# Where the state's decay is applied in a linear-attention and mixture kernel, and in what order its start is laid out

## The chip, the cores and the metric

One core of a Trainium2 chip runs the whole program. The metric is the device time of one execution in microseconds (us); lower is better. The times named are medians of several runs, and one further execution was taken with the profiler.

## The reference

Three layers follow one another. The first is linear attention with a decaying state, for 2 batches, 8 heads, 768 steps and head size 48. Then come a mixture of 4 experts (384 to 1024 to 384, relu) weighted by normalised probabilities, and one wide layer (384 to 2048 to 384, elu). All is float32.

```python
state = np.zeros((B, H, D, D))
for t in range(S):
    kt, vt, rt = (k[:, :, t], v[:, :, t], r[:, :, t])
    cur = np.einsum('bhd,bhe->bhde', u[None] * kt, vt)
    y[:, :, t] = np.einsum('bhd,bhde->bhe', rt, state + cur)
    state = w[None, :, :, None] * state + np.einsum('bhd,bhe->bhde', kt, vt)
...
p = domain_probs / (domain_probs.sum(-1, keepdims=True) + 1e-09)
for e in range(E):
    h = np.maximum(x @ w1[e], 0.0)
    out += p[:, e:e + 1] * (h @ w2[e])
...
h = x @ w_in
g = np.where(h > 0.0, h, np.exp(np.minimum(h, 0.0)) - 1.0)
return g @ w_out
```

The decays w lie between 0.85 and 0.95.

## The kernel before, in words

**The attention** (class Fast) cuts the 1536 steps into 12 chunks of 128, six for each batch. Two tables are made at the start: T holds the powers of w from 0 to 128 (T[:, :, P:P + 1] is w to the 128th), Kd their reciprocals. Receptances are multiplied by T and keys by Kd (s1h, VectorE, L206), so that within a chunk the decay falls out of the product (s2, TensorE, L263). VectorE's copy_predicated (s2p, L270) writes the causal part of it into a tile A that GpSimd (L242) or ScalarE (s1e, L248) has filled with the diagonal term of u. The chunk's own sum over keys and values (s3u, TensorE, L285) goes into a bank pu, with keys from kp, which GpSimd makes in s1k (L216) from the table Kt. Kt is Kd transposed on TensorE (setup_kt, L199) and copied by ScalarE (L200). VectorE then makes the state (s3s): for chunk 0 it multiplies pu by w to the 128th into the padded tile Sp (L302); afterwards it adds the old state to pu (Z, L309) and multiplies by w to the 128th (S, L311). Chunk 1 takes its state from Sp (s3f, L375), later chunks from S (s3, L325), and s3 adds the products of A and v (L334); ScalarE copies the result to yT (L341).

**The layers** (class Gen) work in float32 split in two parts, high and low: ScalarE casts the high part and another engine subtracts it. For weights these are wh (ScalarE, L532) and wl (VectorE, sometimes GpSimd, L533), for activations xh and xl (L495, L496), for the hidden values hh and hl (L696, L697). A group is a first product into a bank ph (st1, L684), its evacuation to hh and hl, and, two groups later, a second product (st2, L722). For the first 1024 steps a group has 256 columns and the two banks ph0 and ph1 take turns (new_ph, counter nph).

**The order.** The program is scheduled by hand: each engine gets its instructions in the order in which the program issues them. The function fast writes that order out: the warm-up matmuls on a tile of zeros (warm, L102), zeros, loads, tables, the first two chunks, and then the layers, between whose groups the steps of the later chunks are dealt out by hand. After the first group (f=0) come a1(2), probs2 and a2(3), after the second a3(2), after the third a1p(3), after the fourth a3(3). After each group's steps, work() issues one split of a weight slice: wh on ScalarE, wl on VectorE. So a3(2), which holds s3s(2), stands before the split of the second group on both engines.

Of the kernel before, what the change touches and what calls it, by code (L numbers as in the profile page):

```python
# [10 lines left out]
F32 = mybir.dt.float32  # L11
# [5 lines left out]
AF = mybir.ActivationFunctionType  # L17
ALU = mybir.AluOpType
# [4 lines left out]
P = 128  # L23
B, H, S, D = 2, 8, 768, 48
NP = H // 2
NCB = S // P
# [8 lines left out]
WARM = 18  # L35
# [15 lines left out]
class Fast:  # L51
# [7 lines left out]
    def __init__(self, g, ctx):  # L59
        self.g, nc, tc = g, g.nc, g.tc  # L60
        self.c = ctx.enter_context(tc.tile_pool(name="at_c", bufs=1))
        self.p2 = ctx.enter_context(tc.tile_pool(name="at_2", bufs=2))
        self.p3 = ctx.enter_context(tc.tile_pool(name="at_3", bufs=3))
        self.p4 = ctx.enter_context(tc.tile_pool(name="at_4", bufs=4))
        self.ps = ctx.enter_context(tc.tile_pool(name="at_ps", bufs=1, space=PSUM))
        c = self.c
        self.A = [c.tile([P, 2, NP, P], F32, name=f"A{i}") for i in range(2)]
        self.kp = [c.tile([P, NP, 2, 64], F32, name=f"kp{i}") for i in range(2)]
        self.Sb = [c.tile([P, NP, 64], F32, name=f"S{i}") for i in range(2)]
        self.wd = c.tile([P, NP], F32, name="wd")  # L70
        self.T = c.tile([P, NP, P + 1], F32, name="T")
        self.Kd = c.tile([P, NP, P], F32, name="Kd")
        self.Kt = c.tile([P, NP, 2, 64], F32, name="Kt")
        self.ub = c.tile([P, DM], F32, name="ub")
        self.ur = c.tile([1, DM], F32, name="ur")
        self.one = c.tile([1, P], F32, name="one")
        self.vp = c.tile([P, 112 + 160 * H], F32, tag="xs", name="vp")
        self.Sp = c.tile([P, 96 + 192 * NP], F32, tag="yT", name="Sp")
        self.mask = c.tile([P, P], U8, name="mask")
        self.rkT, self.rk, self.v, self.va, self.pa, self.st, self.px = ({} for _ in range(7))  # L80
        self.S = self.Sv = self.zero = None

        self.own = [(self.ps, f"pa{i}") for i in range(3)] + [(g.pop, "po2")]
        self.banks = self.own[:3] + [(g.pop, f"po{i}") for i in range(KD)] + [(g.php, "ph0")]
        self.nbank = 0
        self.xd = g.dr.tile([DM, N], F32, name="xd")
# [108 lines left out]
    def setup_kt(self):  # L195
        g, nc = self.g, self.g.nc
        pk = self.bank()
        for p in range(NP):
            nc.tensor.transpose(pk[:, p * P:(p + 1) * P], self.Kd[:, p, :], g.ident)  # L199
        nc.scalar.copy(self.Kt.rearrange("t p j d -> t (p j d)"), pk)  # L200


# [87 lines left out]
    def s3s(self, ci, pu):  # L290
        nc = self.g.nc
        if pu is None:
            return
        old, v = self.Sv, nc.vector
        w = self.T[0:112, :, P:P + 1]
        src = pu[0:112, 0:NP * D].rearrange("q (p e) -> q p e", p=NP)
        if not ci:
            self.Sv = self.Sp[0:112, 96:].rearrange("q (p n) -> q p n", p=NP)[:, :, 0:96].rearrange(
                "q p (j e) -> q p j e", j=2)
            for j in range(2):  # L300
                a = slice(64 * j, 64 * j + D)
                v.tensor_tensor(out=self.Sv[a, :, j, :], in0=src[a], in1=w[a].to_broadcast([D, NP, D]), op=ALU.mult)  # L302
            return
        self.S = self.Sb[ci % 2]
        self.Sv = self.S[0:112, :, 0:D]
        if ci % NCB:
            z = self.p2.tile([P, NP, D], F32, tag="Z", name="Z")[0:112]
            for a, o in [(slice(0, 64), old[:, :, 0]), (slice(64, 112), old[:, :, 1])] if ci == 1 else [(slice(0, 112), old)]:
                v.tensor_tensor(out=z[a], in0=src[a], in1=o[a], op=ALU.add)  # L309
            src = z  # L310
        v.tensor_tensor(out=self.Sv, in0=src, in1=w.to_broadcast([112, NP, D]), op=ALU.mult)  # L311

    def s3(self, ci, more=False):
        g, nc = self.g, self.g.nc
        st = self.st.pop(ci)
        A, v, c = self.A[ci % 2], self.v[ci], ci % NCB
        py = [self.bank()[:, 0:2 * P].rearrange("q (s t) -> q s t", s=2) for j in range(2)]
        heads = [(p, j) for q in range(2) for p in (q, q + 2) for j in range(2)]
        at = lambda p, j, m: py[j][64 * (p // 2):64 * (p // 2) + m, p % 2, :]


        if c:
            for p, j in heads:
                a, m = 64 * j, D if p // 2 else 64
                nc.tensor.matmul(  # L325
                    at(p, j, m), self.S[a:a + D, p, 0:m], st["r"][a:a + D, p, :], start=not p % 2, stop=False)
        if more:
            self.s2(ci + 1)
        pu = self.s3u(ci, g.new_ph() if ci > 2 else g.pop.tile([P, TB], F32, tag="po1", name="po1")) if c < NCB - 1 else None
        for j in range(2):  # L330
            for p in (0, 2, 1, 3):

                h, m = 2 * p + j, D if c or p // 2 else 64
                nc.tensor.matmul(  # L334
                    at(p, j, m), v[:, h * D:h * D + m], A[:, j, p, :], start=not c, stop=not c or p % 2 == 1)
        self.s3s(ci, pu)
        o = (ci % 2) * P
        if not o:
            self.yT = self.c.tile([P, 2, 2, 2 * P], F32, tag="yT", name="yT")
        for j in range(2):  # L340
            nc.scalar.copy(self.yT[0:112, :, j, o:o + P], py[j][0:112])  # L341
        if o:

            t0 = (ci - 1) * P
            for a in range(2):
                nc.sync.dma_start(
                    out=self.xd[:, t0:t0 + 2 * P].rearrange("(a h e) t -> a e h t", a=2, e=D)[a],
                    in_=self.yT[64 * a:64 * a + D].rearrange("e s j t -> e (s j) t"))
            self.xs = self.c.tile([P, KD, 2 * P], F32, tag="xs", name="xs")
            nc.sync.dma_start(out=self.xs, in_=self.xd[:, t0:t0 + 2 * P].rearrange("(k p) t -> p k t", p=P))  # L350
# [127 lines left out]
class Gen:  # L478
# [378 lines left out]
    def fast(self):  # L857
        tc, nc = self.tc, self.nc
        with ExitStack() as ctx:
# [1 line left out]
            self.hp, self.hw = ctx.enter_context(tc.tile_pool(name="hp", bufs=3)), 256  # L861
            actx = ExitStack()
            at = Fast(self, actx)
            at.warm(WARM - 4)
            at.setup_zeros()
            at.setup_loads()
            dp = self.probs_in()
            make_identity(nc, self.ident)
            self.load_next()
            at.load_rk(2)  # L870
# [2 lines left out]
            at.load_v(2)  # L873
            at.setup_masks()
            at.setup_tables()
            at.setup_rest()
            at.setup_tables2()

            def load(c):
                if c < NCH:  # L880
                    at.load_T(c)
                    at.load_v(c)
# [38 lines left out]
            self.probs(dp)  # L921
            at.s1d(2)
            at.s3s(1, pu)
            self.weng = nc.gpsimd
            self.work(0.1)
            self.weng = nc.vector
            at.banks, at.nbank = at.own, 0
            load(4)
            at.load_rk(4)

# [163 lines left out]
```

## Time and profile before

| | |
|---|---|
| median of 3 runs | 653.62 us (653.33 to 654.23) |
| the profiled execution | 653.03 us |
| its span, first to last instruction | 651.1 us |
| mean granted TensorE clock | 0.997 |
| TensorE / VectorE / ScalarE / GpSimd busy | 639.2 / 334.1 / 216.7 / 214.6 us |

Positions in time are microseconds from the start of the span. PE is TensorE, PEld its weight loads, DVE is VectorE, ACT ScalarE, POOL GpSimd; a q behind the name is the engine's sequencer. In a timeline a line gives the start, the time to the end of the last instruction merged into it, the engine, the line of the program, the operation, the tiles it writes and reads with their shapes, and how many instructions were merged. In brackets stand the idle time ahead of it and what ended it.

### The profile page before, as it was taken

What the parts mean: (1) busy time and instruction counts of PE and PEld (TensorE: products, weight loads), DVE (VectorE), ACT (ScalarE), POOL (GpSimd) and SP (SyncE); (2) the same over time, 40 slices, a digit from 0 to 9 for tenths busy, and PEclk for the clock granted to TensorE, in tenths of its full rate; (3) what the DMA queues carried; (4) which work ended last, traced back from release to release, by engine and by line L of the source; (5) the groups of instructions that cost most, each with busy time, mean ns of one, the idle gap of its engine ahead of it and who ended that gap; (6) DMA issues with size and microseconds to landing.
All of it is one profiled execution on the core that took longest, in us unless ns stands there. A gap on an engine that the chain in (4) does not pass through costs nothing.

```text
span 651.1 us, 9435 instructions
## 1 busy us (share of the span) xinstructions
PE 639.2 (98%) x3825; PEld 537.1 (82%) x3825; DVE 334.1 (51%) x472; ACT 216.7 (33%) x370; POOL 214.6 (33%) x178
## 2 busy tenths in 40 slices
PE   9799999999999999999999999999999999999996
PEld 6699998988888888888888888888888888888885
DVE  7975665346454545554545456566667553222221
ACT  5532222333211132211122112123645564544441
POOL 7954773100031212130311122242754434333331
PEclk9999999999999999999999999999999999999998
DMA  8883562343230233421216231318441342001011
GB/s 257 248 288 120 160 175 76 144 122 122 72 97 1 98 120 118 159 88 48 98 49 229 92 138 52 97 35 312 188 146 44 102 145 98 0 1 49 1 49 53
DMA packets 27735, 73.10 MB, mean 112 GB/s; under 512 B 3154, under 2 KB 8580, under 8 KB 27684
## 3 DMA queue, kind: packets, MB, share of 16 engines
q1 hardware_dynamic: 22928, 59.80, 28.6%
q10 hardware_dynamic: 4756, 12.61, 5.1%
q8 instruction: 32, 0.52, 0.3%
q14 instruction: 19, 0.16, 0.1%
HBM read 55.47 MB, written 16.93 MB: 111 GB/s over the span
## 4 chain that ended last, share of the span: by engine, by line
PE 95%; DVE 3%; issue 1%; ACT 0%; DVEq 0%
PE ph L684 45%; PE po L722 45%; PE pa L263 1%; PE ph L102 1%; PE pa L334 1%; PE pa L325 1%; DVE rkT L206 1%; PE po L334 1%; PE ph L285 1%; DVE A L270 0%; DVE wl L533 0%; DVE a L232 0%; DVE acc L772 0%; DVE hl L697 0%; DVE xl L496 0%
## 5 line engine op out<-in xcount | busy, mean ns | idle before, releaser
L722 PE MATMUL po<-hh,wh 128*128 128x512 f32 (+1 forms) x480 | 177.4, 370 | 0.0
L722 PE MATMUL po<-hl,wh 128*128 128x512 f32 (+1 forms) x480 | 176.5, 368 | 0.0
L722 PE MATMUL po<-hh,wl 128*128 128x512 f32 (+1 forms) x480 | 176.5, 368 | 0.0
L684 PE MATMUL ph<-xh,wh 128*128 128x512 f32 (+1 forms) x480 | 174.5, 369 | 1.5 <-DVE xl L496 0.8
L684 PE MATMUL ph<-xh,wl 128*128 128x512 f32 (+1 forms) x480 | 173.8, 368 | 0.0
L696 ACT ACTIVATE hh<-ph 128x512 fp32r<-128x512 f32 (+1 forms) x112 | 60.2, 537 | 269.3 <-PE ph L684 266.4
L697 DVE SCALAR_TENSOR_TENSOR hl<-ph,hh 128x512 fp32r<-128x512 f32 (+1 forms) x112 | 68.5, 613 | 154.6 <-ACT hh L696 154.2
L684 PE MATMUL ph<-xl,wh 128*128 128x512 f32 (+1 forms) x480 | 124.6, 368 | 0.0
L684 PEld LDWEIGHTS ph<-xh,wh 128*128 128x128 f32 x480 | 90.4, 188 | 17.6 <-DVE hl L697 1.0
L722 PEld LDWEIGHTS po<-hh,wh 128*128 128x128 f32 x480 | 90.4, 188 | 16.5 <-issue 1.5
L722 PEld LDWEIGHTS po<-hl,wh 128*128 128x128 f32 x480 | 90.4, 188 | 15.0
L722 PEld LDWEIGHTS po<-hh,wl 128*128 128x128 f32 x480 | 90.4, 188 | 15.0
L684 PEld LDWEIGHTS ph<-xh,wl 128*128 128x128 f32 x480 | 90.5, 188 | 14.9
L709 POOL TENSOR_TENSOR hl<-g,hh 128x512 fp32r<-128x512 f32 x48 | 63.2, 1318 | 117.4 <-ACT hh L708 109.3
L684 PEld LDWEIGHTS ph<-xl,wh 128*128 128x128 f32 x480 | 85.9, 188 | 15.2 <-DVE xl L496 0.2
L595 POOL TENSOR_TENSOR nl<-a,wide 128x768 fp32r<-128x768 f32 x16 | 29.9, 1870 | 173.5 <-issue 105.8
L706 DVE SCALAR_TENSOR_TENSOR g<-m,ph 128x512 f32<-128x512 f32 x48 | 33.0, 686 | 104.4 <-ACT m L704 100.1
L744 POOL TENSOR_TENSOR acc<-acc,t 128x512 f32<-128x512 f32 x27 | 34.2, 1297 | 72.8 <-DVE t L743 72.8
L708 ACT CAST hh<-g 128x512 fp32r<-128x512 f32 x48 | 29.9, 622 | 43.0 <-DVE g L706 43.0
L703 ACT ACTIVATE m<-ph 128x512 f32<-128x512 f32 x48 | 28.7, 598 | 43.4 <-PE ph L684 36.4
L533 DVE TENSOR_TENSOR wl<-raw,wh 128x768 fp32r<-128x768 f32 x31 | 30.7, 1004 | 7.2 <-ACT wh L532 6.7
L704 ACT ACTIVATE m<-m 128x512 f32<-128x512 f32 x48 | 30.4, 632 | 1.5
(116 smaller groups left out, 478.9 us busy)
## 6 DMA issues: line engine op xcount, KB each, us to landing
raw<-in_ws_dram SPq DMA_DIRECT2D x32, 384.0 KB, 4.3
wide<-in_ws_dram SPq DMA_DIRECT2D x16, 768.0 KB, 5.1
w<-nh ACTq DMA_DIRECT2D x16, 384.0 KB, 2.5
w<-nl ACTq DMA_DIRECT2D x16, 384.0 KB, 5.6
wh<-w SPq DMA_DIRECT2D x16, 384.0 KB, 6.0
wl<-w SPq DMA_DIRECT2D x16, 384.0 KB, 6.8
rk<-in_rkv_dram SPq DMA_DIRECT2D x12, 384.0 KB, 6.4
rkT<-in_rkT_dram SPq DMA_DIRECT2D x10, 448.0 KB, 6.0
```

Source lines behind the costliest of these rows:

```text
L533: self.weng.tensor_tensor(out=lo, in0=t, in1=hi.bitcast(F32), op=ALU.subtract)
L595: nc.gpsimd.tensor_tensor(out=lo, in0=af, in1=cf, op=ALU.add)
L684: nc.tensor.matmul(ph[:, 0:n], a[:, kk, c0:c0 + P], b[:, kk], start=q == 0, stop=q == 3 * KD - 1)
L696: nc.scalar.activation(hh[:, 0:n], ph[:, 0:n], AF.Relu)
L697: nc.vector.scalar_tensor_tensor(out=hl[:, 0:n], in0=ph[:, 0:n], scalar=0.0, in1=hh[:, 0:n].bitcast(F32), op0=ALU.max, op1=ALU.subtract)
L703: nc.scalar.activation(m, ph, AF.Relu, scale=-1.0)
L704: nc.scalar.activation(m, m, AF.Exp, scale=-1.0)
L706: nc.vector.scalar_tensor_tensor(out=gg, in0=m, scalar=-1.0, in1=ph, op0=ALU.add, op1=ALU.max)
L708: nc.scalar.copy(hh, gg)
L709: nc.gpsimd.tensor_tensor(out=hl, in0=gg, in1=hh.bitcast(F32), op=ALU.subtract)
L722: nc.tensor.matmul(po, a[:, ff, i * P:(i + 1) * P], b[:, 0:n], start=f == 0 and q == 0 and not i * n % TB, stop=f == NF - 1 and q == 2 and ...
L744: nc.gpsimd.tensor_tensor(out=a, in0=a, in1=t[:, 0:n], op=ALU.add)
```

## The change

The state is written as decay times old state plus a sum that already holds the decays. For that, the keys' table Kt is made from T in reverse (w to the power 127 - t for step t) instead of from Kd, through a reversed copy Tr on ScalarE. A new function s3w makes wS, the old state times w to the 128th, with four scaled ACTIVATEs on ScalarE; VectorE's s3s then needs one add of pu and wS. For chunk 0 ScalarE copies pu into Sp and scales it straight from the bank. For chunk 6, which begins the second batch, VectorE copies pu. s3w is issued after s3s for chunk 1, and in s3 after the two copies to yT for the first four chunks of a batch. GpSimd's clearing of its tiles (setup_rest) is issued ahead of the identity and the masks. The warm-up has 10 matmuls instead of 14 (WARM is 18). The counter nph starts the layers at 1, in bank ph1.

```diff
@@ -78,7 +78,7 @@
         self.Sp = c.tile([P, 96 + 192 * NP], F32, tag="yT", name="Sp")
         self.mask = c.tile([P, P], U8, name="mask")
         self.rkT, self.rk, self.v, self.va, self.pa, self.st, self.px = ({} for _ in range(7))
-        self.S = self.Sv = self.zero = None
+        self.S = self.wS = self.zero = None
 
         self.own = [(self.ps, f"pa{i}") for i in range(3)] + [(g.pop, "po2")]
         self.banks = self.own[:3] + [(g.pop, f"po{i}") for i in range(KD)] + [(g.php, "ph0")]
@@ -195,8 +195,10 @@
     def setup_kt(self):
         g, nc = self.g, self.g.nc
         pk = self.bank()
+        Tr = self.c.tile([P, NP, P], F32, name="Tr")
+        nc.scalar.copy(Tr, self.T[:, :, P - 1::-1])
         for p in range(NP):
-            nc.tensor.transpose(pk[:, p * P:(p + 1) * P], self.Kd[:, p, :], g.ident)
+            nc.tensor.transpose(pk[:, p * P:(p + 1) * P], Tr[:, p, :], g.ident)
         nc.scalar.copy(self.Kt.rearrange("t p j d -> t (p j d)"), pk)
 
 
@@ -291,24 +293,27 @@
         nc = self.g.nc
         if pu is None:
             return
-        old, v = self.Sv, nc.vector
-        w = self.T[0:112, :, P:P + 1]
         src = pu[0:112, 0:NP * D].rearrange("q (p e) -> q p e", p=NP)
         if not ci:
-            self.Sv = self.Sp[0:112, 96:].rearrange("q (p n) -> q p n", p=NP)[:, :, 0:96].rearrange(
+            Sv = self.Sp[0:112, 96:].rearrange("q (p n) -> q p n", p=NP)[:, :, 0:96].rearrange(
                 "q p (j e) -> q p j e", j=2)
             for j in range(2):
                 a = slice(64 * j, 64 * j + D)
-                v.tensor_tensor(out=self.Sv[a, :, j, :], in0=src[a], in1=w[a].to_broadcast([D, NP, D]), op=ALU.mult)
+                nc.scalar.copy(Sv[a, :, j, :], src[a])
+            self.s3w(src)
             return
         self.S = self.Sb[ci % 2]
-        self.Sv = self.S[0:112, :, 0:D]
+        out = self.S[0:112, :, 0:D]
         if ci % NCB:
-            z = self.p2.tile([P, NP, D], F32, tag="Z", name="Z")[0:112]
-            for a, o in [(slice(0, 64), old[:, :, 0]), (slice(64, 112), old[:, :, 1])] if ci == 1 else [(slice(0, 112), old)]:
-                v.tensor_tensor(out=z[a], in0=src[a], in1=o[a], op=ALU.add)
-            src = z
-        v.tensor_tensor(out=self.Sv, in0=src, in1=w.to_broadcast([112, NP, D]), op=ALU.mult)
+            nc.vector.tensor_tensor(out=out, in0=src, in1=self.wS, op=ALU.add)
+        else:
+            nc.vector.tensor_copy(out, src)
+
+    def s3w(self, src):
+        self.wS = self.p2.tile([P, NP, D], F32, tag="wS", name="wS")[0:112]
+        for p in range(NP):
+            self.g.nc.scalar.activation(
+                self.wS[:, p, :], src[:, p, :], AF.Copy, scale=self.T[0:112, p, P:P + 1])
 
     def s3(self, ci, more=False):
         g, nc = self.g, self.g.nc
@@ -339,6 +344,8 @@
             self.yT = self.c.tile([P, 2, 2, 2 * P], F32, tag="yT", name="yT")
         for j in range(2):
             nc.scalar.copy(self.yT[0:112, :, j, o:o + P], py[j][0:112])
+        if c < NCB - 2:
+            self.s3w(self.S[0:112, :, 0:D])
         if o:
 
             t0 = (ci - 1) * P
@@ -861,10 +868,11 @@
             self.hp, self.hw = ctx.enter_context(tc.tile_pool(name="hp", bufs=3)), 256
             actx = ExitStack()
             at = Fast(self, actx)
-            at.warm(WARM - 4)
+            at.warm(WARM - 8)
             at.setup_zeros()
             at.setup_loads()
             dp = self.probs_in()
+            at.setup_rest()
             make_identity(nc, self.ident)
             self.load_next()
             at.load_rk(2)
@@ -873,7 +881,6 @@
             at.load_v(2)
             at.setup_masks()
             at.setup_tables()
-            at.setup_rest()
             at.setup_tables2()
 
             def load(c):
@@ -921,10 +928,11 @@
             self.probs(dp)
             at.s1d(2)
             at.s3s(1, pu)
+            at.s3w(at.S[0:112, :, 0:D])
             self.weng = nc.gpsimd
             self.work(0.1)
             self.weng = nc.vector
-            at.banks, at.nbank = at.own, 0
+            at.banks, at.nbank, self.nph = at.own, 0, 1
             load(4)
             at.load_rk(4)
```

## Rows read from the trace of the kernel before

**Rows 1.** The page, engines: busy us, share of the span, instructions.
```profile
PE 639.2 (98%) x3825; PEld 537.1 (82%) x3825; DVE 334.1 (51%) x472; ACT 216.7 (33%) x370; POOL 214.6 (33%) x178
```

**Rows 2.** By stretch: length; busy PE, PEld, DVE, ACT, POOL; granted clock, DMA, GB/s.
```profile
5.00:12.00 7.00, 7.00 (x116) 4.87 (x114) 5.81 (x11) 2.20 (x5) 4.62 (x6) 1.00 1.02 345
12.00:20.00 8.00, 5.97 (x78) 5.31 (x77) 7.87 (x10) 3.32 (x6) 7.76 (x8) 1.00 1.05 243
20.00:30.00 10.00, 8.13 (x140) 6.90 (x140) 9.89 (x18) 6.54 (x16) 9.15 (x9) 1.00 0.70 232
...
50.00:100.00 50.00, 49.98 (x719) 47.14 (x712) 30.37 (x59) 11.60 (x29) 32.00 (x29) 1.00 0.51 148
```

**Rows 3.** Waits of TensorE, 0 to 50: waiter, waited for, us, times, longest.
```profile
PE ph L684 <- DVE xl L496: 0.8, 1, 0.8
...
PE ph L684 <- DVE hl L697: 0.6, 1, 0.6
```

**Rows 4.** Timeline of TensorE, 0 to 45.
```profile
6.46 0.91 PE L192 MATMUL ph<-ur,one 1*128 1x384 f32 x2
7.30 0.66 PE L199 MATMUL pa<-ident,Kd 128*128 128x128 f32 x4
...
20.29 1.10 PE L263 MATMUL pa<-rkT 48*64 48x128 f32 x32 [1.07 <-issue]
...
30.39 0.39 PE L684 MATMUL ph<-xh,wh 128*128 128x256 f32 x1 [0.56 <-DVE hl L697]
```

**Rows 5.** Timeline of ScalarE, 0 to 34.
```profile
7.41 0.48 ACT L193 COPY ub<-ph 128x384 f32<-128x384 f32 x1 [1.78 <-PE ph L192]
7.99 0.59 ACT L200 COPY Kt<-pa 128x512 f32<-128x512 f32 x1
...
16.89 0.83 ACT L532 CAST wh<-raw 128x768 fp32r<-128x768 f32 x1
19.25 0.38 ACT L696 ACTIVATE hh<-ph 128x256 fp32r<-128x256 f32 x1 [1.53 <-PE ph L684]
20.68 1.28 ACT L248 ACTIVATE A<-ident,a 128x128 f32<-128x128 f32 x4 [1.05 <-DVE a L232]
...
25.06 0.84 ACT L532 CAST wh<-raw 128x768 fp32r<-128x768 f32 x1
```

**Rows 6.** Timeline of VectorE, 0 to 34.
```profile
11.61 0.70 DVE L302 TENSOR_TENSOR Sp<-po,T 48x192 f32<-48x192 f32 x2
...
15.41 1.76 DVE L533 TENSOR_TENSOR wl<-raw,wh 128x768 fp32r<-128x768 f32 x1
...
20.57 0.71 DVE L309 TENSOR_TENSOR Z<-pa,Sp 64x192 f32<-64x192 f32 x2
21.32 0.74 DVE L311 TENSOR_TENSOR S<-Z,T 112x192 f32<-112x192 f32 x1
22.09 0.42 DVE L697 SCALAR_TENSOR_TENSOR hl<-ph,hh 128x256 fp32r<-128x256 f32 x1
...
28.27 0.34 DVE L309 TENSOR_TENSOR Z<-po,S 112x192 f32<-112x192 f32 x1
28.65 0.48 DVE L311 TENSOR_TENSOR S<-Z,T 112x192 f32<-112x192 f32 x1
29.05 0.94 DVE L533 TENSOR_TENSOR wl<-raw,wh 128x768 fp32r<-128x768 f32 x1
```

**Rows 7.** Timeline of TensorE's weight loads, 0 to 9.
```profile
5.41 0.15 PEld L102 LDWEIGHTS <-zero 128*128 128x128 bf16 x1 [0.27 <-issue]
```

**Rows 8.** Instructions of line 192: ns min/median/max, first and last start.
```profile
L192 PEldq EVENT_SEMAPHORE  x1: 51/51/51, 5.1 to 5.1; - x1
```

**Rows 9.** Timeline of GpSimd, 0 to 34.
```profile
4.69 1.85 POOL L159 TENSOR_TENSOR Kd<-Kd 128x64 f32<-128x64 f32 x3 [1.30 <-DVE Kd L150]
...
15.03 1.32 POOL L223 TENSOR_TENSOR uk<-rk,ub 128x384 f32<-128x384 f32 x1
```

**Rows 10.** Instructions of line 248: ns min/median/max, first and last start.
```profile
L248 ACT ACTIVATE A<-ident,a x8: 386/386/403, 20.7 to 28.1; 128x128 f32<-128x128 f32 x8
```

## The prediction

> **What bounds the kernel now.** I read the page first: TensorE is busy for 98% of 651.1 us [rows 1]. So only two things can change the time: the few microseconds in which TensorE stands idle, and its own warm-up work. The table by stretches shows where the idle time is. From 50 to 100 us TensorE is busy throughout; from 12 to 30 us it is not (5.97 of 8 us, then 8.13 of 10), and there VectorE is busy 7.87 of 8 and 9.89 of 10 [rows 2]. The list of waits agrees: TensorE waits for VectorE's xl and hl [rows 3]. So until about 30 us VectorE's queue sets the pace, and from the start of the fourth group of the layers, at 30.39, TensorE runs on by itself [rows 4]. I count the change by how much that start at 30.39 moves. Every engine takes its instructions in program order, so the timelines of ScalarE and VectorE show what stands behind what.
>
> ScalarE has slack in this stretch, but of a special kind: it runs ahead. It casts the split of the second group (wh) at 25.06, while VectorE, which has that work queued behind its state update, comes to it only at 29.05 [rows 5, 6]. That lead is what the change spends.
>
> **The head.** Four of 14 warm-up matmuls go. Weight loads run one ahead, and the twelfth is at 5.41 [rows 7], so ten matmuls are through there and the product that spreads u could start at about 5.45 instead of 6.46 [rows 4]; its input was there, since the sequencer passed its semaphore at 5.1 [rows 8]. Gain 1.0 us. But the key table now needs a reversed copy on ScalarE, queued behind the copy of ub, which waits for that product: the product takes 0.91, ub's copy 0.48 and the new copy of 512 columns about what Kt's took, 0.59 [rows 4, 5]. With 0.05 for each hand-over this is 5.45 + 0.91 + 0.48 + 0.59 = 7.43, so the transposes start at about 7.45 instead of 7.30: +0.15. The trace has no reversed read; I bound the copy by the shortest and the longest copy shown, 0.48 and 0.83 [rows 5], and take 0.59, since Kt's has the same width. Without the shorter warm-up the same copy would cost 1.0 more.
>
> GpSimd clears its tiles before it makes identity and mask instead of after: the same instructions in another order. They are hidden by its wait for VectorE's reciprocal, which ended at 4.69 after 1.30 us idle [rows 9]; without that cover a shift could cost at most as much as the clears take. The other bank for the first group lets TensorE start it without waiting for xl (0.8 us [rows 3]), but TensorE then waits for VectorE's keys at 20.29 anyway, after 1.07 us idle [rows 4]. Both at nothing.
>
> **What VectorE saves.** The first state was scaled by two instructions (0.70 together); ScalarE now copies it. The second took 0.71 (two adds) and 0.74; one add remains. The third took 0.34 and 0.48; one add remains [rows 6]. The add that remains reads a PSUM bank and an SBUF tile as those of 0.34 to 0.36 did, so I take 0.36. The 0.70 at 11.61 hardly counts: VectorE's next long work, the split at 15.41, took 1.76 where the same form takes 0.94 at 29.05, while a product of 1.32 us ran on GpSimd from 15.03 [rows 6, 9]. If GpSimd sets the end of that split, an earlier VectorE only waits longer; if not, up to 0.70 - 0.15 = 0.55 is won. The Trainium skill ("SBUF — State Buffer", "SBUF: two separate sides") says that VectorE and GpSimd share one port pair as an exclusive lock for a whole instruction, which would explain the 1.76. By that rule the gain here is nothing and the sum further down 2.6; by the row of 0.94 alone it would be 2.05.
>
> **What ScalarE gets.** Each scaling of a state is four ACTIVATEs over 48 columns with a scale from a tile. The same operation over 128 columns took 386 ns, and four of them 1.28 us, so one starts 0.298 after the other [rows 5, 10]. Copies of 512 and 384 columns (0.59 and 0.48) give 0.86 ns a column; 80 columns fewer make 0.317 and a spacing of 0.23, so four take 3 x 0.23 + 0.317 = 1.0 us. Bounds: 0.7 at a spacing of half, 1.28 as measured for 128 columns. For the first state these fall into ScalarE's idle time before 16.89 and cost nothing; for chunks 6 to 9, beyond 50 us, ScalarE is busy 11.60 of 50 and TensorE waits for nothing [rows 2].
>
> For the second and third state they do not fall into idle time. In program order the scaling stands on ScalarE behind VectorE's new state and in front of ScalarE's own next casts.
>
> Second state: VectorE starts the add at 20.57 as before and ends it at 20.93, 1.12 us earlier than 22.05 [rows 6]. ScalarE waits for it, though it had gone on at 16.89 before. Then come the scaling (1.0), wh of the next split (0.83, overlapped 0.09), and only then hh of the first group (0.38), which was done at 19.25 before [rows 5]. VectorE needs hh for hl. So hl starts at about 20.93 + 1.0 + 0.74 + 0.29 + 0.09 = 23.05 instead of 22.09: **+0.96**. Behind hh stands also the diagonal that VectorE's second masked copy needs (1.28 us [rows 5] from about 22.92, so done at 24.2). VectorE, after hl and the first masked copy, is there about as early: I count +0.2, and TensorE's attention product of chunk 2 waits with it.
>
> Third state: VectorE comes to it 1.16 later and saves 0.34 + 0.48 - 0.36 = 0.46, so the state is done at 29.13 + 0.70 = 29.83. ScalarE, which had run ahead, now waits there: scaling 1.0, then wh 0.83 less 0.09, so VectorE's split of that wh starts at 29.83 + 1.0 + 0.74 + 0.09 = 31.66 instead of 29.05 [rows 5, 6]. **The lead that ScalarE had is used up, and VectorE stands idle in its turn**: +2.6 for hl behind it, and with it for the fourth group of TensorE, which needs that hl's bank.
>
> Sum: between 2.05 (if the 0.55 is kept) and 2.6, with the head's 0.15 hidden behind GpSimd or not. I take **+2.4 us**. Later it should neither grow nor be given back: beyond 50 us TensorE waits for next to nothing [rows 2], so no stall is left there that the delay could eat. The scaling of chunk 3 again puts 1 us ahead of a split, but TensorE needs that one only two groups later. The profiled execution took 653.03 us for a span of 651.1; it becomes 655.4. The median of 653.62 lies 0.6 above the profiled execution, and so becomes 656.0.
>
> **The rivals.** The measurement can hardly tell less than 0.2%, 1.3 us.
>
> *As forecast, ScalarE held back* (0.70): 656.0. With the scaling at 0.7 or 1.28 twice and the reversed copy at 0.83, the sum goes from 1.3 to 3.9: 654.9 to 657.5.
>
> *VectorE's relief carries* (0.08), the other side: faster. VectorE saves 1.12 and 0.46, 1.58 by 30 us; less 0.15 for the head this gives 652.2. For it speaks that VectorE is the full engine and that ScalarE idles for 1.5 us before hh at 19.25 and 1.05 before 20.68. The point that decides: scaling and wh fit in front of hh at 19.25 only if the second state is ready by 19.25 - 1.0 - 0.74 = 17.5. Against it, two key products and a reduction stand in front of it on VectorE, and the add could start only at 20.57.
>
> *Collisions with GpSimd fall away* (0.11): about the same time. The split at 15.41 took 0.82 more than the one at 29.05 [rows 6]. Should the shift pull two such pieces apart from GpSimd's, 2 x 0.8 comes back: +0.8, 654.4. Against it: GpSimd's work shifts with VectorE's, as its inputs come through the same waits.
>
> *TensorE falls to its lower clock* (0.11). At 5.41 the warm-up's 512 columns still come every 0.42 us (0.27 idle and 0.15 of a load [rows 7]), 1.2 columns per ns, the lower level, though the granted clock reads 1.00 in every stretch shown [rows 2]. With ten, the warm-up ends at about 5.5 and TensorE then idles for a microsecond. From 5 to 12 TensorE works without a gap [rows 2]; if the higher level is missed from 8 to 12, 4 us of products take 8: with the forecast's 2.4 that is +6.4 at most, 660.0, and half of it 658. The Trainium skill ("TensorE: Matmul & The Clock Gate", "Part 1: The HAM clock gate") says that the slow level is the default, that activity releases it and that idleness brings it back. Nothing in this trace shows a fall during the work: TensorE was busy only 8.13 of 10 us from 20 to 30 and the clock stayed [rows 2].
>
> **The numbers.** Slower by over 1.3 us: 0.67 of the forecast's 0.70 and all of the clock's 0.11, 0.78; the same: 0.10 of the collisions and 0.03 of the forecast, 0.13; faster 0.09 (the relief's 0.08, and 0.01 of the collisions). The range leaves out the relief and the most favourable collisions below (0.12) and the full loss of the clock above (0.08): 654.3 to 658.9.
>
> **What the changed profile would show.** Right: ScalarE's scaling of the second state begins with a wait for VectorE of about 3 us; hh of the first group starts after 22 us; VectorE, without gaps before, has idle time of about 2 us before hl and again before the split of the third state's group, both ended by ScalarE; the fourth group starts near 32.8. Wrong: hh of the first group before 20 us, or VectorE without gaps. The head is right if the transposes start at 7.4 to 7.6. The prediction fails if ScalarE's order differs from the program's, if the four scalings are far from 1.0, or if matmuls after 5.5 us stay at the wide spacing.

## The result, and the profile after

The changed kernel takes 658.39 us (median of 9 runs, 657.03 to 660.11) where the kernel before takes 653.62 (9 runs): a ratio of 1.0073, interval 1.006 to 1.0086, or 4.8 us more. Forecast were 2.4 more, 656.0, in a range of 654.3 to 658.9. The sign and the place were right; half of the amount came from what the forecast held for a rival.

The page of the changed kernel: busy time of the engines, and the granted clock in 40 slices of 16.4 us. VectorE's busy time fell by 9 us against [rows 1], and TensorE's rose, though it has four warm-up matmuls fewer. In the clock's row 9 is full speed: the first slice has a 7 and the third an 8, so in both the clock was below it for a part.

```profile
PE 642.5 (98%) x3821; PEld 540.8 (82%) x3821; DVE 325.2 (50%) x461; ACT 224.1 (34%) x405; POOL 212.0 (32%) x178
...
PEclk7989999999999999999999999999999999999999
```

ScalarE's timeline. The lines have moved: L199 is the reversed copy, L315 the scaling, L539 wh, L703 hh, L250 the diagonal.

```profile
6.48 0.62 ACT L199 COPY Tr<-T 128x512 f32<-128x512 f32 x1
...
22.34 1.01 ACT L315 ACTIVATE wS<-S,T 112x48 f32<-112x48 f32 x4 [2.55 <-DVE S L308]
23.27 0.82 ACT L539 CAST wh<-raw 128x768 fp32r<-128x768 f32 x1
23.99 0.37 ACT L703 ACTIVATE hh<-ph 128x256 fp32r<-128x256 f32 x1
24.26 1.27 ACT L250 ACTIVATE A<-ident,a 128x128 f32<-128x128 f32 x4
...
30.95 1.01 ACT L315 ACTIVATE wS<-S,T 112x48 f32<-112x48 f32 x4 [3.50 <-DVE S L308]
31.87 0.81 ACT L539 CAST wh<-raw 128x768 fp32r<-128x768 f32 x1
```

VectorE's timeline, L308 being the one add that is left of the state, L704 hl and L540 the split.

```profile
21.96 0.35 DVE L308 TENSOR_TENSOR S<-pa,wS 112x192 f32<-112x192 f32 x1
24.39 0.42 DVE L704 SCALAR_TENSOR_TENSOR hl<-ph,hh 128x256 fp32r<-128x256 f32 x1 [2.08 <-ACT hh L703]
...
30.52 0.34 DVE L308 TENSOR_TENSOR S<-po,wS 112x192 f32<-112x192 f32 x1
32.72 1.42 DVE L540 TENSOR_TENSOR wl<-raw,wh 128x768 fp32r<-128x768 f32 x1 [1.86 <-ACT wh L539]
34.06 0.41 DVE L704 SCALAR_TENSOR_TENSOR hl<-ph,hh 128x256 fp32r<-128x256 f32 x1
```

The two timelines are one loop: ScalarE stands still until VectorE has the state, and VectorE, which had no gap at these places before [rows 6], then stands still until ScalarE has scaled it and made the next cast. The two gaps of VectorE, 2.08 and 1.86, were forecast from single rows as 2.12 and 1.83.

What was not in the forecast's sum stands in the busy time by stretch (the columns are those of [rows 2]) and in TensorE's timeline (L201 the transposes, L691 and L729 a group's first and second product).

```profile
5.20:8.10 2.90, 1.72 (x19) 0.97 (x22) 1.78 (x4) 1.61 (x5) 0.81 (x1) 1.00 0.93 279
8.10:14.90 6.80, 6.80 (x108) 6.45 (x100) 5.37 (x9) 2.41 (x8) 5.88 (x6) 0.50 1.05 344
...
30.00:35.40 5.40, 2.34 (x24) 2.03 (x18) 3.54 (x7) 4.07 (x12) 5.14 (x5) 1.00 1.03 321
35.40:38.80 3.40, 3.40 (x45) 2.85 (x46) 2.09 (x4) 0.38 (x1) 0.58 (x1) 0.50 0.79 256
```

```profile
5.16 0.91 PE L192 MATMUL ph<-ur,one 1*128 1x384 f32 x2
7.25 0.63 PE L201 MATMUL pa<-ident,Tr 128*128 128x128 f32 x4 [1.18 <-ACT Tr L199]
...
34.53 0.39 PE L691 MATMUL ph<-xh,wh 128*128 128x256 f32 x1 [2.45 <-DVE hl L704]
...
39.36 0.39 PE L729 MATMUL po<-hh,wh 128*128 128x256 f32 x1
```

Twice TensorE was granted half its clock, 1.2 instead of 2.4 GHz: from 8.1 to 14.9, after a stretch in which it was busy 1.72 of 2.90 us, and from 35.4 to 38.8, after one of 2.34 of 5.40. The fourth group starts at 34.53 instead of 30.39 [rows 4], 4.14 later. From its start to the second product that follows it, 4.83 us go by.

The two stretches are not an accident of the profiled execution. Each run lists its mean granted clock: 0.989 to 0.995 in the nine runs of the changed kernel, with a median of 0.990, and 0.997 or more in 28 of the 29 runs of the kernel before that were taken with the first experiments. Half the clock for 10.2 us (6.8 and 3.4) is 0.8% of the span, about that difference.

### The profile page after: what moved, and what is told of

Same layout as the page of the kernel before. It is cut to its first block, busy times and chain, and to the rows that moved or that the text cites. A ratio compares the mean times of both kernels' runs of the same rounds, so it can differ in the third digit from the quotient of the medians.

```text
span 656.1 us, 9458 instructions
## 1 busy us (share of the span) xinstructions
PE 642.5 (98%) x3821; PEld 540.8 (82%) x3821; DVE 325.2 (50%) x461; ACT 224.1 (34%) x405; POOL 212.0 (32%) x178
## 4 chain that ended last, share of the span: by engine, by line
PE 96%; DVE 2%; ACT 1%; issue 1%; DVEq 0%; ACTq 0%
PE ph L691 45%; PE po L729 45%; PE pa L265 1%; PE pa L339 1%; PE pa L330 1%; PE ph L287 1%; PE ph L102 1%; PE po L339 1%; DVE rkT L208 0%; ACT wS L315 0%; PE pa L382 0%; DVE acc L779 0%; PE po L265 0%; ACT wh L539 0%; ACT xh L502 0%
## 5 line engine op out<-in xcount | busy, mean ns | idle before, releaser
L729 PE MATMUL po<-hh,wh 128*128 128x512 f32 (+1 forms) x480 | 177.5, 370 | 0.0
L691 PE MATMUL ph<-xh,wh 128*128 128x512 f32 (+1 forms) x480 | 174.6, 369 | 2.6 <-DVE hl L704 2.5
L729 PE MATMUL po<-hl,wh 128*128 128x512 f32 (+1 forms) x480 | 176.6, 368 | 0.0
L729 PE MATMUL po<-hh,wl 128*128 128x512 f32 (+1 forms) x480 | 176.6, 368 | 0.0
L691 PE MATMUL ph<-xh,wl 128*128 128x512 f32 (+1 forms) x480 | 173.8, 368 | 0.0
L703 ACT ACTIVATE hh<-ph 128x512 fp32r<-128x512 f32 (+1 forms) x112 | 60.1, 536 | 266.0 <-PE ph L691 262.5
L704 DVE SCALAR_TENSOR_TENSOR hl<-ph,hh 128x512 fp32r<-128x512 f32 (+1 forms) x112 | 68.4, 613 | 162.4 <-ACT hh L703 162.0
L691 PE MATMUL ph<-xl,wh 128*128 128x512 f32 (+1 forms) x480 | 124.9, 369 | 0.0
L691 PEld LDWEIGHTS ph<-xh,wh 128*128 128x128 f32 x480 | 90.4, 188 | 18.7 <-DVE hl L704 2.7
L729 PEld LDWEIGHTS po<-hh,wh 128*128 128x128 f32 x480 | 90.4, 188 | 16.5 <-issue 1.5
L729 PEld LDWEIGHTS po<-hl,wh 128*128 128x128 f32 x480 | 90.4, 188 | 15.0
L691 PEld LDWEIGHTS ph<-xh,wl 128*128 128x128 f32 x480 | 90.5, 188 | 14.9
L729 PEld LDWEIGHTS po<-hh,wl 128*128 128x128 f32 x480 | 90.4, 188 | 14.9
L691 PEld LDWEIGHTS ph<-xl,wh 128*128 128x128 f32 x480 | 86.0, 189 | 15.2 <-DVE xl L503 0.2
L540 DVE TENSOR_TENSOR wl<-raw,wh 128x768 fp32r<-128x768 f32 x31 | 30.5, 997 | 8.6 <-ACT wh L539 8.1
```

The source lines that it names most:

```text
L540: self.weng.tensor_tensor(out=lo, in0=t, in1=hi.bitcast(F32), op=ALU.subtract)
L691: nc.tensor.matmul(ph[:, 0:n], a[:, kk, c0:c0 + P], b[:, kk], start=q == 0, stop=q == 3 * KD - 1)
L703: nc.scalar.activation(hh[:, 0:n], ph[:, 0:n], AF.Relu)
L704: nc.vector.scalar_tensor_tensor(out=hl[:, 0:n], in0=ph[:, 0:n], scalar=0.0, in1=hh[:, 0:n].bitcast(F32), op0=ALU.max, op1=ALU.subtract)
L729: nc.tensor.matmul(po, a[:, ff, i * P:(i + 1) * P], b[:, 0:n], start=f == 0 and q == 0 and not i * n % TB, stop=f == NF - 1 and q == 2 and ...
```

## The experiments

Ratios are to the kernel before, run beside each. Where two experiments are compared in us, the difference of their ratios is multiplied by 654; each such difference is uncertain by about 1.2 us (an estimate from the intervals). "The changed kernel" has 1.0073. The expectations number the kernels in the order of running: the second is "The scaling late", the sixth the second state alone, the seventh the last one of "The head".

**The scaling late.** The same instructions, but each scaling issued at the start of the next chunk's step, behind ScalarE's casts.

```diff
     def s3(self, ci, more=False):
         ...
+        if 0 < c < NCB - 1:
+            self.s3w(self.S[0:112, :, 0:D])
         heads = ...
         ...
-        if c < NCB - 2:
-            self.s3w(self.S[0:112, :, 0:D])
...
             at.s3s(1, pu)
-            at.s3w(at.S[0:112, :, 0:D])
```

> The changed kernel with the scaling of a state issued at the start of the next chunk's step instead of right behind the state: the same instructions, but on ScalarE behind the casts that VectorE and TensorE need first. Theory A (ScalarE's queue held back costs some 2.5 us, and the idle time of TensorE that it makes brings the second stretch at the lower clock, another 1.5): both go, VectorE has no gap before hl and before the split of the third state's group, the clock stays at 1.00 near 36 us, and the time is 653 to 655. Rival C (the loss is all of the warm-up and the clock; ScalarE's waits are hidden): 657 to 659.

Measured: 654.12 us, ratio 1.0004, interval 0.9994 to 1.0014. 4.5 us come back by moving the call. VectorE's timeline of this kernel:

```profile
20.92 0.34 DVE L308 TENSOR_TENSOR S<-pa,wS 112x192 f32<-112x192 f32 x1
21.18 0.41 DVE L704 SCALAR_TENSOR_TENSOR hl<-ph,hh 128x256 fp32r<-128x256 f32 x1
22.22 1.38 DVE L272 COPY_PREDICATED A<-mask,pa 128x512 f32<-128x512 uint8 x2 [0.63 <-POOL A L244]
...
26.87 0.55 DVE L234 TENSOR_REDUCE a<-uk 128x8 f32<-128x384 f32 x1 [0.91 <-POOL uk L227]
...
28.54 0.35 DVE L308 TENSOR_TENSOR S<-po,wS 112x192 f32<-112x192 f32 x1
28.81 1.20 DVE L540 TENSOR_TENSOR wl<-raw,wh 128x768 fp32r<-128x768 f32 x1
```

Both gaps behind ScalarE are gone: hl and the split follow the state at once. So the place in ScalarE's queue, not the scaling itself, costs the time. But the kernel is not faster than the one before, although VectorE has some 1.5 us less to do: two new gaps, 0.63 and 0.91, are ended by GpSimd. Its profile also has a stretch at half the clock, from 7.5 to 10.9, which could be a second reason. The last kernel of "The head" has none there, keeps both gaps, and is not clearly faster either.

**One state at a time.** First the second state's scaling alone is moved, then all but that.

```diff
+        if ci == 2:
+            self.s3w(self.S[0:112, :, 0:D])
...
-            at.s3w(at.S[0:112, :, 0:D])
```

> The changed kernel with the scaling of the second state alone moved behind the casts of the first two groups; that of the third state stays where the change put it. Theory A in its terms (about 1.2 for the second state's scaling, 1.4 and the slow stretch near 36 us for the third's): 1.2 comes back, the gap ahead of hl of the first group goes, the gap ahead of the split behind the third state and the slow stretch stay, 656.8 to 657.5. Rival E (one of the two places carries it all, the other hides in it): 658.4 if the third does, 654 to 654.5 if the second does.

Measured: 656.54 us, 1.0045, interval 1.0029 to 1.006.

```diff
+        if 0 < c < NCB - 1 and ci != 2:
+            self.s3w(self.S[0:112, :, 0:D])
...
-        if c < NCB - 2:
-            self.s3w(self.S[0:112, :, 0:D])
```

> The changed kernel with all scalings late but that of the second state. With the sixth kernel this gives the two terms apart: the third state's scaling was priced 1.4 (forecast) and the slow stretch near 36 us 1.5. Theory A: the gap ahead of the split behind the third state and the slow stretch go, the gap ahead of hl of the first group stays, 655.2 to 656. If the second state's hold-up is enough to bring a slow stretch by itself, 656.5 or more.

Measured: 655.46 us, 1.0016, interval 1.0001 to 1.0031. VectorE's timelines, of the kernel with the second state's scaling late, and then of the one with the others late:

```profile
21.11 0.41 DVE L706 SCALAR_TENSOR_TENSOR hl<-ph,hh 128x256 fp32r<-128x256 f32 x1
...
30.62 1.47 DVE L542 TENSOR_TENSOR wl<-raw,wh 128x768 fp32r<-128x768 f32 x1 [1.80 <-ACT wh L541]
```

```profile
23.77 0.42 DVE L704 SCALAR_TENSOR_TENSOR hl<-ph,hh 128x256 fp32r<-128x256 f32 x1 [2.08 <-ACT hh L703]
...
30.16 1.20 DVE L540 TENSOR_TENSOR wl<-raw,wh 128x768 fp32r<-128x768 f32 x1
```

Each move takes away its own gap and leaves the other, 1.80 and 2.08. The first gives 1.8 us back, the second 3.7; priced were 1.2 and 2.9 (with the stretch at the lower clock). Together they would be 5.5, and both at once gave 4.5, which the uncertainty allows. With the third state's scaling in its place the clock still falls, here to half from 32.8 to 36.2, after 0.36 us of work in 2.80:

```profile
30.00:32.80 2.80, 0.36 (x3) 0.32 (x3) 2.18 (x3) 2.80 (x8) 2.53 (x3) 1.00 0.99 279
32.80:36.20 3.40, 3.40 (x41) 2.85 (x40) 2.37 (x4) 0.50 (x2) 1.12 (x2) 0.50 0.95 291
```

With the others late the clock stays at 1.00 from 30 to 40, as expected, but the profile has a stretch at half the clock elsewhere, behind a wait of 1.59 us for ScalarE's cast of the next inputs:

```profile
47.84 0.39 PE L691 MATMUL ph<-xh,wh 128*128 128x256 f32 x1 [1.59 <-ACT xh L502]
48.90:52.30 3.40, 3.40 (x16) 3.40 (x17) 1.88 (x4) 0.38 (x1) 1.71 (x2) 0.50 1.02 398
```

The kernel before with ten warm-up matmuls (below) has a wait of 1.63 for the same cast and keeps the full rate behind it, so a wait of this length does not always bring the fall.

**The wait filled.** Nothing waits less, but TensorE works while it waits: nine matmuls on zeros in front of the fourth group.

```diff
             def before(u, t0, f):
+                if (u, t0, f) == (0, 0, 3):
+                    pz = at.bank()
+                    at.nbank -= 1
+                    for _ in range(9):
+                        nc.tensor.matmul(pz, at.zero[:, 0:P], at.zero, start=True, stop=True)
```

> The changed kernel with nine further matmuls on the tile of zeros, issued on TensorE ahead of the fourth group, where it waits some 2.5 us for VectorE; their result is never read. Theory A (the stretch at the lower clock near 36 us comes from TensorE's idle time in that wait, and costs about 1.5): the clock stays at 1.00 there and the time falls to 656.5 to 657.5, though nothing else waits less. Rival D (that stretch is chance, or costs nothing): 658.4 as before, or more by what the nine matmuls take.

Measured: 655.62 us, 1.0033, interval 1.002 to 1.0047; 2.6 us less than the changed kernel. TensorE's timeline (of the nine matmuls it has eight records) and its busy time by stretch:

```profile
30.78 2.12 PE L998 MATMUL pa<-zero 128*128 128x512 bf16 x8
33.66 0.39 PE L691 MATMUL ph<-xh,wh 128*128 128x256 f32 x1 [0.77 <-DVE hl L704]
...
36.99 0.38 PE L729 MATMUL po<-hh,wh 128*128 128x256 f32 x1
```

```profile
30.00:35.40 5.40, 4.58 (x41) 3.08 (x41) 3.83 (x5) 4.17 (x13) 4.57 (x5) 1.00 0.95 289
35.40:38.80 3.40, 3.40 (x55) 3.10 (x48) 1.20 (x3) 2.14 (x8) 0.00 (x0) 1.00 0.78 245
```

With 4.58 of 5.40 us busy the clock stays at 1.00, and from the group's start to the second product it takes 3.33 us instead of 4.83. So the second stretch at the lower clock came from TensorE's idle time and cost 1.5 us. The other profiles bear this out: in all five kernels in which TensorE stood in this wait, for 2.36 to 2.63 us, the clock fell during it or within 1.5 us of its end; in the six in which the wait is gone or filled it reads 1.00 from 30 to 40. The group's own start, 33.66 instead of 34.53, is earlier for another reason: in this execution the early stretch at the lower clock was shorter. That explains the part of the 2.6 above 1.5. It holds for the median too, as five of the seven runs lie within 0.2 us of it and list a mean clock of 0.994 to 0.996, like the profiled one (0.995); the two of 657.5 list 0.997. Why the early stretch was shorter, with a head that the edit leaves alone, is open.

**The head.** Three kernels: the changed one with 14 warm-up matmuls, the kernel before with ten, and "The scaling late" (ten) with the reversed copy moved ahead of ub's copy as well, so that the transposes need not wait for it.

```diff
-            at.warm(WARM - 8)
+            at.warm(WARM - 4)
```

> The changed kernel with the warm-up of 14 matmuls that the kernel before had. Theory A: the early stretch at the lower clock (8.6 to 15.4 us, granted clock 0.53) came from the shorter warm-up, which leaves TensorE idle before the higher level is secured. Then that stretch is gone, some 1.4 us come back there, about 1.0 is lost in the head because the transposes wait for the copy that waits for the product behind the warm-up, and the time is 657.5 to 658.5. The later slow stretch near 36 us stays, since ScalarE's waits stay. Rival B: it came from the gap of 1.18 us ahead of the transposes, whatever the warm-up's length. Then the slow stretch stays as well and the time is 659 to 660.

Measured: 659.06 us, 1.0085, interval 1.0069 to 1.0101.

```diff
-            at.warm(WARM - 4)
+            at.warm(WARM - 8)
```

> The kernel before with ten warm-up matmuls instead of 14 and nothing else. Theory A: the shorter warm-up alone is enough to lose the higher clock for a stretch after 8 us, and the time is 654.5 to 656, for the product of u comes 1.0 earlier but the products up to 15 us take twice as long. Rival B (it takes the gap ahead of the transposes too): the clock stays at 1.00, the head is up to 0.6 earlier, and the time is 652.8 to 653.6.

Measured: 654.5 us, 1.0013, interval 1.0001 to 1.0024. In the third diff only the copy's move is shown; the scaling's move is the one above.

```diff
             at.s1h(0, 1)
+            at.setup_tr()
             at.setup_ub()
...
+    def setup_tr(self):
+        self.Tr = self.c.tile([P, NP, P], F32, name="Tr")
+        self.g.nc.scalar.copy(self.Tr, self.T[:, :, P - 1::-1])
```

> As the second kernel of this call, and the reversed copy of the table is issued on ScalarE ahead of the copy of u's product, so that the transposes do not wait for that product. Theory A (a short warm-up alone): a stretch at the lower clock remains after 8 us and the time is near the second kernel's, 653 to 654.5. Rival B (the gap): the gap ahead of the transposes is gone, the clock stays, and with the head 0.5 earlier the time is 651 to 652.5.

Measured: 652.78 us, 0.9994, interval 0.9979 to 1.0008. The changed kernel with 14 warm-up matmuls, by stretch; then TensorE's timeline of the kernel before with ten, and of the kernel with the copy first:

```profile
5.20:8.10 2.90, 1.73 (x7) 0.51 (x5) 2.24 (x4) 1.43 (x4) 0.82 (x1) 1.00 0.96 310
8.10:14.90 6.80, 6.28 (x112) 5.55 (x112) 3.63 (x6) 2.91 (x10) 4.85 (x5) 0.75 1.05 343
```

```profile
7.12 1.11 PE L199 MATMUL pa<-ident,Kd 128*128 128x128 f32 x4
8.17 1.99 PE L263 MATMUL pa<-rkT 48*64 48x128 f32 x32
```

```profile
6.96 1.10 PE L267 MATMUL pa<-rkT 48*64 48x128 f32 x32
8.79 1.95 PE L267 MATMUL po<-rkT 48*64 48x128 f32 x32 [0.73 <-DVE rkT L210]
```

The longer warm-up does not keep the changed kernel's clock: it falls at 8.1 again, for half of the stretch, and the time is rival B's. All six runs list a mean clock of 0.989 to 0.993; the second stretch alone would leave about 0.995 (an estimate: half of 3.4 us in 656 below the kernel before's 0.998). With ten and no gap the kernel before runs its transposes in 1.11 us instead of 0.66 and its first key products in 1.99 instead of 1.10, so here the higher level had not come, though the profile's clock reads 1.00. With the copy first the transposes wait for nothing, but TensorE waits 0.73 for VectorE's keys, and the clock falls behind that. So either edit alone was enough, in the one or two profiles that have it alone.

> The changed kernel with the scaling late, the reversed copy ahead of the copy of u's product, and a warm-up of 14. If the longer warm-up secures the higher clock at the start, it keeps the relief of VectorE (1.5) with the head of the kernel before: 652 to 653, with less spread over the runs than with ten. If the early slow stretch comes by chance with either warm-up, it is no better than with ten, 652.5 to 653.5, since TensorE then starts its first products 0.5 later.

Measured, with 14 matmuls, the copy first and the scaling late (the edits above): 653.24 us, 0.9992, interval 0.9982 to 1.0003. TensorE and VectorE in its profile:

```profile
20.30 1.10 PE L267 MATMUL pa<-rkT 48*64 48x128 f32 x32 [1.51 <-DVE rkT L210]
20.59 0.34 DVE L310 TENSOR_TENSOR S<-pa,wS 112x192 f32<-112x192 f32 x1
```

The profile shows 1.00 throughout the start, and the first key products take 1.10, the full rate, but the median is no better than with ten. In the profile TensorE then waits 1.51 us for VectorE's keys of chunk 2. And this profile, with a mean clock of 0.999, is not typical: six of the eleven runs list 0.994 to 0.996, under the 0.997 and more of the 18 runs of the kernel before beside them, so a stretch at the lower level is left somewhere in those.

**GpSimd as the next in the chain.** From the last kernel, the split of the second weight slice goes to VectorE.

```diff
-            self.weng = nc.gpsimd
             self.work(0.1)
-            self.weng = nc.vector
```

> As the seventh kernel (scaling late, reversed copy first, 14 warm-up matmuls), and the split of the second weight slice, 1.83 us on GpSimd, is done by VectorE instead. Theory F: with ScalarE out of the way VectorE's relief of 1.5 was not paid out because GpSimd became the next in the chain (VectorE waited 0.9 for its product uk and 0.6 for its diagonal). Then the wait for uk goes, the fourth group starts 0.6 to 1.0 earlier, and the time is 652.2 to 652.8, clearly under the kernel before. Rival G: the split takes VectorE what the wait gave it, and the time is that of the seventh kernel, 653.0 to 653.5.

Measured: 652.41 us, 0.9974, interval 0.9959 to 0.9989: faster than the kernel before by about 1.7 us, the only one whose interval lies below 1. Against the kernel that it starts from (0.9992) it gains 1.2 us, no more than the uncertainty. VectorE's reduction for chunk 3 no longer waits, but a later split now waits for ScalarE:

```profile
25.84 0.75 DVE L210 TENSOR_TENSOR rkT<-rkT,Kd 112x512 f32<-112x512 f32 x1
26.51 0.54 DVE L236 TENSOR_REDUCE a<-uk 128x8 f32<-128x384 f32 x1
...
29.53 1.08 DVE L542 TENSOR_TENSOR wl<-raw,wh 128x768 fp32r<-128x768 f32 x1 [1.01 <-ACT wh L541]
```

The profiled execution, 653.63 us, is not typical of it: the clock fell in it where it had not before, after a stretch of 2.33 busy in 3.70 us, and its mean clock of 0.993 is the lowest that the twelve runs list.

```profile
17.00:20.70 3.70, 2.33 (x27) 1.73 (x25) 3.70 (x5) 1.62 (x4) 3.58 (x4) 1.00 1.04 279
20.70:27.60 6.90, 6.70 (x80) 5.84 (x82) 6.30 (x12) 3.28 (x10) 5.37 (x7) 0.51 0.68 218
```

So the earlier start of the fourth group cannot be read from it. That the kernel is faster than the kernel before rests on the medians; that GpSimd's wait was what held it back is argued from the wait that is gone, not shown.

**The two edits priced at nothing**, in the changed kernel:

```diff
-            at.banks, at.nbank, self.nph = at.own, 0, 1
+            at.banks, at.nbank = at.own, 0
```

> The changed kernel with the layers beginning in the first bank, as in the kernel before. By the prediction the other bank is worth nothing, since TensorE waits for VectorE's keys right after: 658 to 659. Rival: the earlier start of the first group is kept, and its loss shows as 0.7 more, 659.

Measured: 657.95 us, 1.0054, interval 1.0039 to 1.0069.

```diff
-            at.setup_rest()
             make_identity(nc, self.ident)
             ...
             at.setup_tables()
+            at.setup_rest()
```

> The changed kernel with GpSimd's clears behind the masks again, as in the kernel before. By the prediction their order is worth nothing: 658 to 659. Rival: the order moves the identity and the mask enough to matter at the start, 0.5 either way beyond the spread.

Measured: 658.83 us, 1.0081, interval 1.0061 to 1.0101. Both intervals hold or touch the changed kernel's; with four runs each, nothing under 1 us can be told. The traces tell more about the clears. VectorE's first work on the decays in the changed kernel, the same with the clears behind the masks, and GpSimd's clear of Sp in the latter:

```profile
2.37 0.31 DVE L144 TENSOR_SCALAR wf<-wd 128x4 f32<-128x4 f32 x1 [1.07 <-DMA wd<-in_wd_dram]
2.39 1.02 DVE L144 TENSOR_SCALAR wf<-wd 128x4 f32<-128x4 f32 x1 [1.09 <-DMA wd<-in_wd_dram]
2.38 0.82 POOL L186 MEMSET Sp<- 128x864 f32 x1
```

Beside that clear the small instruction took 1.02 us instead of 0.31, and VectorE's reciprocal starts at 4.04 instead of 3.52. In the three profiles with the clears behind the masks it takes 0.83 to 1.02, in the other ten 0.17 to 0.31. So the order is worth about 0.5 us to the start of VectorE's tables, where the prediction had nothing; in the time it does not show.

## Why the prediction was right in sign and short by half

**The head.** Right in its steps, not in its start: the reversed copy took 0.62 against 0.59 in the sum, but the product of u starts at 5.16, 1.3 earlier than before where 1.0 (5.45) was forecast. So the transposes start at 7.25, outside the 7.4 to 7.6 that the prediction had named as its sign, and 0.05 earlier than before instead of 0.15 later. That the head leaves TensorE idle was seen; what it does to the clock was not in the sum.

**VectorE's saving and ScalarE's scaling.** Right: the add took 0.35 (0.36 forecast), four scalings 1.01 (1.0). The upper end of the forecast's own bounds, 3.9, is too high for the terms that it names: 2.6, twice 0.28 for the scalings, 0.24 for the reversed copy and 0.15 for the head make 3.55. Single ones of line 315:

```profile
L315 ACT ACTIVATE wS<-S,T x12: 320/322/338, 22.3 to 40.4; 112x48 f32<-112x48 f32 x12
```

**ScalarE held back.** Right as a mechanism and in size. From the second state's end (22.31) to the fourth group (34.53) the trace has 12.2 us; the forecast had 11.9 (20.93 to 32.8). The 0.3 more is made of three parts: the split behind the third state took 0.48 longer (1.42 instead of 0.94), the third state came 0.35 sooner after the second than counted, and the forecast had taken 2.4 where this chain by itself gave 2.6. The experiment with the scaling late shows that this order is the cause.

**The failed step** is that the lower clock was held for a rival: it stood as a case of its own, chance 0.11, with the shorter warm-up and the idle microsecond behind it as its only source, and the forecast's 2.4 was summed at full clock. Both came together, and the prediction's own sign for it, matmuls at the wide spacing after 5.5, was there from 8.1 on. Without the clock's case the forecast's own bounds end at 657.5, so 658.39 lies in the stated range only through that case. That its middle, 658, comes so near is luck, for it was the 2.4 and an early loss of 2.0, where the traces have 1.4 early and 1.5 later. The early stretch, the forecast's fourth rival, put the second state 1.38 later than forecast (22.31 against 20.93); in the kernel with 14 matmuls and the copy first, which keeps its clock there, the add starts at 20.59 where 20.57 was forecast. The second stretch the prediction did not see at all: the wait that it forecast for TensorE is itself idle time, and the clock fell behind it, 1.5 us. The account by the traces: 1.4 early clock, 2.4 forecast and 0.3 more for the held-back queue, 1.5 for the second stretch, 5.6 at 39.36; the span is only 5.0 longer, mostly because a wait of 0.5 that TensorE had once beyond 50 us in the kernel before does not occur. "So no stall is left there that the delay could eat" was thus wrong by that 0.5.

The argument that the clock would stay, TensorE being busy only 8.13 of 10 us before without a fall, was too coarse: in the changed kernel it was busy 8.25 of 10 from 20 to 30, and fell behind the 5.4 us that followed, with 2.34. The Trainium skill ("TensorE: Matmul & The Clock Gate", "HAM oscillation — how this bites in real kernels") says that waits between bursts of matmuls bring the slow level back again and again. The traces agree in kind, as the three stretches shown above tell: TensorE was busy 1.72 of 2.90, 2.34 of 5.40 and 2.33 of 3.70 us, and each was followed by a granted 0.50 or 0.51.

**The relief rival** (652.2) was wrong for a second reason that the prediction did not give: with ScalarE out of the way two waits for GpSimd, 0.63 and 0.91, are as long together as VectorE's saving, and 654.12 was measured. With a piece of GpSimd's work gone as well 652.41 was measured; that the waits are the reason is argued, since that last step is within the uncertainty.

**Open:** how much of the early stretch is the shorter warm-up's and how much the gap's. In the ten profiles with either or both, TensorE works at half its rate for a stretch between 7 and 16 us; in the three with neither (the kernel before, and the two kernels with 14 matmuls and the copy first) it does not. But the stretch's length differs, 3.4 to 6.8 where the profile records it, and one profile a kernel does not price the two apart. Idle time alone does not settle it either: the kernel before, busy 2.97 of 4.60 us from 15.4 to 20, kept its clock.

## What to carry to other kernels

Before work moves to an engine with idle time, look at why it is idle: an engine that runs ahead of the one it feeds is idle and still sets the pace as soon as an instruction in its queue waits for the slower one. Such work belongs behind the casts that others wait for, as late as its own reader allows. And a wait that empties TensorE should be priced twice, once for its length and once for the clock after it, which here cost 1.5 us behind a wait of 2.45.

## What the runs showed of the hardware that was not expected

A wait of 2.45 us in an otherwise dense stream (2.34 busy of 5.40) was enough for the granted clock to fall to 0.50, for 3.4 us of work that then took 1.5 longer, and nine matmuls whose result is never read bought that back. The granted clock reads 1.00 from the start in the profile, while warm-up matmuls of 512 columns came every 0.43 us, the lower level. In the kernel before with ten of them it still reads 1.00 while the key products take 1.99 us instead of 1.10. So a 1.00 ahead of the first change that the profile records does not tell the level; the spacing does. A copy that reads its rows backwards on ScalarE costs about as much as a straight one: 0.62 us for 512 columns, against 0.59 for Kt's, which reads a PSUM bank. An instruction of VectorE over 4 columns took 1.02 us instead of 0.31 beside GpSimd's clear of Sp.
